# Other block sizes and a crossbar transpose for group 3 in a fused attention and SwiGLU kernel

## The chip, the cores and the metric

The kernel runs on one core of one Trainium2 chip. A core has TensorE (PE in the profile; its weight loads are PEld), VectorE (DVE), ScalarE (ACT), GpSimd (POOL) and SyncE (SP). Each takes its instructions in the order of the program. DMA transfers are issued by SP, ACT or POOL and run on 16 shared DMA engines. The metric is device time in microseconds (us) of one execution; lower is better.

## The reference

Attention with a window of 128 and 4 sink tokens, for 4 batches, 8 heads, 768 positions and a head size of 64; its output, as 3072 tokens of 512, goes through a gated layer with 1536 hidden units.

```python
scores = scale * np.matmul(q, k.transpose(0, 1, 3, 2))
keep = is_sink | in_window          # in_window: 0 <= i - j < 128
scores = np.where(keep, scores, -1000000000.0)
a = np.exp(scores - max);  a = a / (sum + 1e-09)
x = np.matmul(a, v)                 # heads side by side: 3072 x 512
g = x @ w_gate
out = (g * (1.0 / (1.0 + np.exp(-g))) * (x @ w_val)) @ w_out
```

Inputs and output are float32; the kernel computes in bfloat16 with float32 sums.

## The kernel before, in words

**Two tilings.** The attention goes by 12 *groups* of 256 positions, three for each batch (group 3 begins batch 1, group 6 batch 2, group 9 batch 3). The gated layer goes by 8 *blocks* of tokens, whose lengths stand in `SIZES` (L42): 256, 256, 256, 512, 512, 512, 512, 256. A block needs the output of the groups that hold its tokens: block 3 (512) that of groups 3 and 4, block 4 that of 5 and 6, and so on; block 7 (256) that of group 11.

**Attention of a group g.** Keys and queries are loaded as they lie (`load_nat`, four DMAs on POOL's queue, L113) and must be turned so that the head size lies on the partitions. Groups 2 and 3 are turned on TensorE by `step_TN` (L279, four transposes into one PSUM bank `pn`, then a copy by ACT or DVE); from group 4 on by DMA transposes (`xbar`, L293, four issued by SP). The tile that `load_nat` fills has one buffer from group 4 on, so a load waits for the transposes of the group before. `load_v` loads the values. Then:

- `step_S1` (L360): the score matmuls (L382, tile `s`, six PSUM banks), for groups that don't begin a batch also the scores against the sinks (`mm_K`, L432, tile `pk`; with `apart` in `step_S2` instead), three exponentials on ACT (L395) and the first of four masks.
- `step_S2`: three more exponentials, that of the sinks (`es`, L438), and the second mask. `step_S3`: masks 3 and 4. A mask is a multiplication on DVE (L404) over the probabilities `e` of two heads: masks 1 and 2 for heads 0 to 3, masks 3 and 4 for heads 4 to 7.
- `step_PV`, four times a group: the first also issues `step_sinks` (L454 and, from group 4 on in groups that don't begin a batch, L463, over all eight heads); then L494. Each result `o` holds a PSUM bank until DVE has taken its reciprocal (L503) and scaled it into `xn` (L511).
- `step_X`: turns `xn` into `xT`, the gated layer's input, on TensorE for groups 0 to 2 (L543), by a DMA transpose that SP issues from group 3 on (L538).

**A block** is 12 gate units (6 for a block of 256 alone, 8 shared by blocks 0 and 1) and one down unit for each 128 tokens. `gate` (L611): the projection `pg` (L564), tanh on ACT (L584), the attention steps that share the unit, the projection `pv` (L564), then on DVE `u` (L592) and `ht` (L607, L598, L603). The masks that wait in the list `later` go between and behind these two: one behind `u`, the rest behind `ht`; a `flush` among the steps puts them ahead. A step marked `ahead` (`S1`) is issued before `pg`. `down` (L644): 12 matmuls (L657) into a bank `pd`, among which the steps are spread, then a copy by ACT (L662) and a store (L665), issued by ACT for blocks 0 to 2 and by SP for the others. All PSUM tiles share eight banks (L76).

**The order** is written by hand. `weave` runs a list of units and issues with unit i the steps that `slots` gives for i. `one(at, g)` puts `S1` and `S2` at unit `at` and `S3` at the next. The first `weave` (L860) has 24 units: 0 to 11 the gates of blocks 0 and 1, 12 to 17 the gates of block 2, then two downs each of blocks 0 (18, 19), 1 (20, 21) and 2 (22, 23). Blocks 3, 4 and 5 have a `weave` of 16 units each (0 to 11 gates, 12 to 15 downs) with two groups in it (`pair`, L873), blocks 6 and 7 a last one. For block 3 the first gate is split in two halves of 256 tokens, so that it can start on group 3's half.

**Loads** are ordered by POOL's queue. `behind(tb, t)` and `turned(g)` are copies of one element on POOL (L703, L709) that wait for a token of `xT`, or for the queries of group g, and so hold the loads behind them. POOL issues all weights (L162, L169), the last at about 30 us, then keys, queries and values of group 3.

Of the kernel before, what the change touches and what calls it, by code (L numbers as in the profile page):

```python
# [14 lines left out]
def kernel(  # L15
# [12 lines left out]
    nc = tc.nc  # L28
    P = 128
# [9 lines left out]
    NP2 = H // 2  # L39
    GC = S // 256  # L40
    NG = B * GC
    SIZES = [256, 256, 256, 512, 512, 512, 512, 256]  # L42
    assert sum(SIZES) == NTOK and NG == 12
    OFF = [sum(SIZES[:i]) for i in range(len(SIZES))]
    PEX = (0, 1, 2)
# [477 lines left out]
    def step_X(g, j, evict="v"):  # L523
        t0 = g * 256 + j * P
        tb = max(i for i in range(len(SIZES)) if OFF[i] <= t0)
        off = t0 - OFF[tb]
        if tb == 0 and off == 0:
            xTs["01"] = xtp.tile([P, DMC, 512], BF16, tag="xT", name="xT")
            xTs[0], xTs[1] = (xTs["01"][:, :, 256 * i:256 * (i + 1)] for i in range(2))
        elif tb > 1 and off == 0:  # L530
            xTs[tb] = dense(xtp.tile([P, DMC * 512], BF16, tag="xT", name="xT"),
                            DMC, SIZES[tb])
            if tb == 3:
                for i in range(2):
                    xTs[tb, i] = xTs[tb][:, :, 256 * i:256 * (i + 1)]
        if g not in PEX:
            def sp():
                nc.sync.dma_start_transpose(xTs[tb][:, :, off:off + P], xns[g, j])  # L538
            later.append(sp)
            return  # L540
        pt = bank([P, DMC, P], BF16, "px")
        for i in range(DMC):
            nc.tensor.transpose(pt[:, i], xns[g, j][:, i * P:(i + 1) * P], ident)  # L543

        if evict == "a":
            nc.scalar.copy(out=xTs[tb][:, :, off:off + P], in_=pt)
            return

        def dve():
            nc.vector.tensor_copy(out=xTs[tb][:, :, off:off + P], in_=pt)  # L550
        if evict == "now":
            dve()
        else:
            later.append(dve)
# [89 lines left out]
    def down(tb, ts, attn, last=False):  # L644
        at = {}
        for i, a in enumerate(attn):
            at.setdefault(DFC * (i + 1) // (len(attn) + 1), []).append(a)
        n = DFC // 4
        r0 = OFF[tb] + ts * P
        parts = [(0, 3 * P), (3 * P, DM)] if last else [(0, DM)]  # L650
        for m, (lo, hi) in enumerate(parts):
            po = bank([P, hi - lo], FP32, "pd")
            for f in range(DFC):
                for a in at.get(f, []) if m == 0 else []:
                    a()
                    flush()
                nc.tensor.matmul(  # L657
                    po, hts[tb][:, f, ts * P:(ts + 1) * P], wos[f // n][:, f % n, lo:hi],
                    start=(f == 0), stop=(f == DFC - 1))
            ot = opool.tile([P, hi - lo], FP32, tag=f"ot{hi - lo}", name="ot")  # L660
            if m == 0:
                nc.scalar.activation(ot, po, AF.Copy, scale=0.5)  # L662
            else:
                nc.vector.tensor_scalar(ot, po, 0.5, None, op0=ALU.mult)  # L664
            (nc.scalar if tb < 3 else nc.sync).dma_start(out[r0:r0 + P, lo:hi], ot)  # L665

    def gates(tb):
        return [(gate, tb, f) for f in range(0, DFC, 512 // SIZES[tb])]
# [174 lines left out]
    for f in masks1[:3]:  # L843
# [2 lines left out]
    g0, g1, g2 = gates(0), gates(1), gates(2)  # L846
    us = [(gate_held, *g0[0][1:]), (gate_first, *g0[1][1:]), g1[0], g1[1],
          *((gate, "01", f) for f in range(4, DFC)),
          *g2, *downs(0), *downs(1), *downs(2)]

    def L(*fs):
        def f():
# [4 lines left out]
    def NV(g):  # L857
# [3 lines left out]
        (4, TN(2)[::2]), (5, TN(2)[1::2]), ((6, 7), Ss(2)), (6, [K(2)]),  # L861
        ((8, 8), PVs(2)[:2]), (9, [A(step_PV, 2, 0, 1, "a"), A(step_PV, 2, 1, 1, "a")]),
        ((10, 11), [A(step_X, 2, 0, "a"), ahead(A(step_X, 2, 1, "a"))]),
        (11, [NV(4), lambda: nc.gpsimd.tensor_copy(out=vcl[64:128], in_=vcl[0:64])]),
        ((14, 14, 15, 15), TN(3, "aa")),
        (15, [A(xbar, 4)]), (15, [A(load_nat, 5)]), (19, [A(xbar, 5, (0,))]),
        *one(17, 3), (18, [A(step_ks, 1)]), (18, [A(step_vsb, 1)]),
        ((19, 19, 19, 20), PVs(3)), (19, [S1(4)]), (20, [L(A(step_S2, 4), A(step_S3, 4))]), (20, Xs(3)), (20, [A(xbar, 5, (1,))]),
        ((21, 21, 21, 22), PVs(4)), (21, Xs(4)[:1]),
        (22, [Xs(4)[1], flush, A(behind, 3, 511), A(load_v, 5), A(load_nat, 6)]),  # L870
        (23, [A(xbar, 6), A(turned, 6), A(load_v, 6), NV(7)])))

    def pair(ga, gb, at=0):  # L873
        return [*one(at, ga), ((4, 4, 5, 5), PVs(ga)), ((7, 7), Xs(ga)), *one(8, gb, True),
                ((12, 12, 13, 13), PVs(gb)), ((13, 13), Xs(gb))]

    weave([(gate, (3, i), 0) for i in range(2)] + gates(3)[2:] + downs(3), slots(
        (15, [A(step_ks, 2), A(step_vsb, 2)]), *pair(5, 6), (9, [flush, A(xbar, 7)]),
        (13, [flush, A(behind, 4, 511), NV(8)]),
        (15, [A(xbar, 8)]), (15, [NV(9)])))  # L880
    weave(gates(4) + downs(4), slots(
        *pair(7, 8), (3, [A(xbar, 9)]), (15, [A(step_ks, 3), A(step_vsb, 3)]),
        (3, [A(load_nat, 10)]), (13, [flush, A(behind, 5, 511), A(load_v, 10), NV(11)]),
        (15, [A(xbar, 10)])))
    weave(gates(5) + downs(5), slots(*pair(9, 10), (6, [A(xbar, 11)])))
    us = gates(6) + gates(7) + downs(6) + downs(7)
    us[-1] = (lambda tb, t, a: down(tb, t, a, True), *us[-1][1:])
    weave(us, slots(
        *one(0, 11), ((4, 4, 5, 5), PVs(11)), ((8, 9), Xs(11))))


# [33 lines left out]
```

## Time and profile before

| | us |
|---|---|
| median of 3 runs | 234.16 (233.87 to 234.39) |
| the profiled execution | 233.82 |
| its span, first to last instruction | 231.9 |
| TensorE busy | 225.6 |
| DVE busy | 150.9 |
| ACT busy | 106.4 |
| POOL busy | 84.3 |
| mean granted TensorE clock | 0.993 |

Times in the views count from the start of the span. A row of the timeline gives start, duration, engine, line, operation, what it writes and reads, and how often; in brackets how long the engine had been idle and what ended that. The end of a matmul's row is modelled: rows of matmuls that follow each other overlap by about 0.17 us, and the pieces of the chain of waits give the spacing without the overlap. Rows of DVE and ACT overlap by some 0.1 us in the same way, so that their spacing is taken from the starts. "Busy" of TensorE doesn't mean that every matmul is at its peak.

### The profile page before, as it was taken

What the parts mean: (1) busy time and instruction counts of PE and PEld (TensorE: products, weight loads), DVE (VectorE), ACT (ScalarE), POOL (GpSimd) and SP (SyncE); (2) the same over time, 40 slices, a digit from 0 to 9 for tenths busy, and PEclk for the clock granted to TensorE, in tenths of its full rate; (3) what the DMA queues carried; (4) which work ended last, traced back from release to release, by engine and by line L of the source; (5) the groups of instructions that cost most, each with busy time, mean ns of one, the idle gap of its engine ahead of it and who ended that gap; (6) DMA issues with size and microseconds to landing.
All of it is one profiled execution on the core that took longest, in us unless ns stands there. A gap on an engine that the chain in (4) does not pass through costs nothing.

```text
span 231.9 us, 5433 instructions
## 1 busy us (share of the span) xinstructions
PE 225.6 (97%) x2155; PEld 125.4 (54%) x2155; DVE 150.9 (65%) x327; ACT 106.4 (46%) x212; POOL 84.3 (36%) x123
## 2 busy tenths in 40 slices
PE   7699999999999999999999999999999999999994
PEld 3469645796555644455444454454454544487443
DVE  5878888767660797960797970597960599778000
ACT  4784486566543726423635512835612823333221
POOL 8996874960500907806353415135000000000000
PEclk9979999999999999999999999999999999999999
DMA  8999999999998998998989996989915102000132
GB/s 147 150 185 179 179 198 206 164 156 122 123 154 230 103 134 99 151 195 141 146 119 139 128 124 138 105 109 144 117 40 144 45 3 42 3 3 0 64 120 90
DMA packets 112008, 28.04 MB, mean 121 GB/s; under 512 B 99056, under 2 KB 109040, under 8 KB 111984
## 3 DMA queue, kind: packets, MB, share of 16 engines
q0 software_dynamic: 79904, 14.29, 80.7%
q1 hardware_dynamic: 30672, 11.58, 26.7%
q10 hardware_dynamic: 1408, 1.84, 2.5%
q8 instruction: 17, 0.28, 0.5%
q14 instruction: 7, 0.06, 0.1%
HBM read 29.13 MB, written 6.29 MB: 153 GB/s over the span
## 4 chain that ended last, share of the span: by engine, by line
PE 94%; DMA 2%; POOL 2%; DVE 0%; issue 0%; POOLq 0%
PE pg L564 27%; PE pv L564 27%; PE pd L657 27%; PE o L494 4%; PE s L382 3%; DMA rows<-in_q_dram 2%; PE s L326 1%; PE o L463 1%; PE pk L432 1%; PE pn L279 1%; PE o L454 1%; POOL rows L102 1%; POOL x L216 1%; PE px L543 1%; DVE xT L550 0%
## 5 line engine op out<-in xcount | busy, mean ns | idle before, releaser
L592 DVE SCALAR_TENSOR_TENSOR u<-th,pg 128x512 bf16<-128x512 f32 x72 | 49.2, 683 | 45.4 <-ACT th L584 45.1
L564 PE MATMUL pg<-xT,wg 128*128 128x512 bf16 (+1 forms) x360 | 74.2, 337 | 0.3 <-DVE xT L550 0.3
L564 PE MATMUL pv<-xT,wv 128*128 128x512 bf16 (+1 forms) x360 | 74.1, 336 | 0.0
L584 ACT ACTIVATE th<-pg 128x512 f32<-128x512 f32 x72 | 43.7, 608 | 59.6 <-PE pg L564 59.6
L657 PE MATMUL pd<-wo,ht 128*128 128x512 bf16 (+2 forms) x300 | 65.9, 370 | 0.0
L564 PEld LDWEIGHTS <-wg 128*128 128x128 bf16 x360 | 34.4, 98 | 26.7 <-issue 0.7
L564 PEld LDWEIGHTS <-wv 128*128 128x128 bf16 x360 | 33.9, 98 | 23.5 <-issue 0.2
L607 DVE TENSOR_TENSOR ht<-u,pv 128x512 bf16<-128x512 bf16 x62 | 42.5, 686 | 4.7 <-PE pv L564 0.4
L657 PEld LDWEIGHTS <-ht 128*128 128x128 bf16 x300 | 27.5, 98 | 28.4
L662 ACT ACTIVATE ot<-pd 128x512 f32<-128x512 f32 (+1 forms) x24 | 14.3, 595 | 50.2 <-PE pd L657 46.8
L395 ACT ACTIVATE e<-s 128x512 bf16<-128x512 f32 x54 | 28.5, 614 | 5.8 <-PE s L382 4.9
L113 POOL DMA_DIRECT2D nat<-in_k_dram x20 | 17.7, 895 | 29.3 <-DMA qT<-nat 27.8
L511 DVE TENSOR_TENSOR xn<-o,rcp 128x256 bf16<-128x256 f32 x45 | 17.9, 419 | 0.7
L128 POOL DMA_DIRECT2D vm<-in_v_dram x24 | 17.8, 770 | 1.2 <-DMA va<-in_v_dram 0.7
L113 POOL DMA_DIRECT2D nat<-in_q_dram x20 | 17.8, 906 | 1.0 <-DMA wv<-in_moe_w_val_dram 0.5
L494 PEld LDWEIGHTS <-e 128*128 128x128 bf16 x256 | 12.0, 100 | 6.3 <-issue 0.3
L404 DVE TENSOR_TENSOR e<-e,maskq 128x768 bf16<-128x768 bf16 x24 | 13.1, 553 | 1.9 <-ACT e L395 1.9
L151 POOL DMA_DIRECT2D va<-in_v_dram x12 | 10.7, 917 | 4.3 <-DMA wo<-in_moe_w_out_dram 2.4
L703 POOL CAST warmed<-xT 1x1 f32<-1x1 bf16 x3 | 0.5, 175 | 30.2 <-DMA xT<-xn 30.2
L503 DVE RECIPROCAL rcp<-o 128x4 f32<-128x4 f32 x48 | 7.3, 172 | 5.5 <-PE o L494 5.3
L664 DVE TENSOR_SCALAR ot<-pd 128x128 f32<-128x128 f32 x1 | 0.3, 292 | 14.3 <-PE pd L657 14.3
L333 ACT ACTIVATE e<-s 128x512 bf16<-128x512 f32 x16 | 8.3, 607 | 0.6 <-PE s L326 0.5
(86 smaller groups left out, 138.7 us busy)
## 6 DMA issues: line engine op xcount, KB each, us to landing
out_dram<-ot SPq DMA_DIRECT2D x17, 256.0 KB
nat<-in_k_dram POOLq DMA_DIRECT2D x20, 128.0 KB, 4.7
nat<-in_q_dram POOLq DMA_DIRECT2D x20, 128.0 KB, 4.9
va<-in_v_dram POOLq DMA_DIRECT2D x12, 128.0 KB, 5.9
wg<-in_moe_w_gate_dram POOLq DMA_DIRECT2D x6, 256.0 KB, 7.6
wv<-in_moe_w_val_dram POOLq DMA_DIRECT2D x6, 256.0 KB, 8.2
wo<-in_moe_w_out_dram POOLq DMA_DIRECT2D x4, 384.0 KB, 11.1
out_dram<-ot ACTq DMA_DIRECT2D x6, 256.0 KB
```

Source lines behind the costliest of these rows:

```text
L113: nc.gpsimd.dma_start(x[:, i, j].rearrange("p (h d) -> p h d", d=D), src[b, :, t0:t0 + P].rearrange("h p d -> p h d"))
L128: nc.gpsimd.dma_start(vms[b][p0:p1, t - 1, :, 0:D], v[b, :, t0:t0 + p1 - p0].rearrange("h p d -> p h d"))
L395: nc.scalar.activation(e_t[g][:, e0:e0 + 512], pss[g][w, i], AF.Exp, scale=scale)
L404: nc.vector.tensor_tensor(e, e, m.broadcast_to([P, 2, 384]), op=ALU.mult)
L494: nc.tensor.matmul(o, l, r, start=(c == 0 and i == 0), stop=(i == len(mms) - 1), skip_group_check=True)
L511: nc.vector.tensor_tensor(xn, po[:, :, 0:D], rcp.broadcast_to([P, 4, D]), op=ALU.mult)
L564: nc.tensor.matmul(ps[:, i * n:(i + 1) * n], ws[fi][:, c, fo * P:(fo + 1) * P], xTs[tb][:, c], start=(c == 0), stop=(c == DMC - 1))
L584: nc.scalar.activation(th, pg, AF.Tanh, scale=0.5)
L592: nc.vector.scalar_tensor_tensor(u, th, 1.0, pg, op0=ALU.add, op1=ALU.mult)
L607: nc.vector.tensor_tensor(hts[tb][:, f:f + 512 // SIZES[tb]].rearrange("p a n -> p (a n)"), u, pv, op=ALU.mult)
L657: nc.tensor.matmul(po, hts[tb][:, f, ts * P:(ts + 1) * P], wos[f // n][:, f % n, lo:hi], start=(f == 0), stop=(f == DFC - 1))
L662: nc.scalar.activation(ot, po, AF.Copy, scale=0.5)
```

## The change

- `SIZES` becomes 256, 256, 256, 256, 512, 512, 512, 512: group 3 alone feeds block 3, groups 4 and 5 block 4, up to groups 10 and 11 for block 7. What was said of block 3 (the split first gate) holds for block 4, and ACT issues the stores of block 3 too.
- The first `weave` gets eight more units: 24 to 29 the gates of block 3, 30 and 31 its downs.
- Group 3 is no longer turned by `step_TN` in units 14 and 15: `xbar(3)` is issued on SP in unit 12, and in unit 13 `turned(3)` holds POOL's queue until its queries have landed, with the loads of group 4 behind it (they stood in unit 11).
- Group 3's scores move from unit 17 (a gate) to unit 18 (the first down of block 0), the rest of its exponentials and masks to unit 19. Group 4's scores move from unit 19 to unit 23, its values from 21 and 22 to 25 and 26. Group 5's scores stand in unit 27, its values in 29 and 30; before, they stood in units 0, 4 and 5 of block 3's `weave`.
- From block 4 on each `weave` holds the two groups of the next block: 6 and 7, 8 and 9, 10 and 11. The last block's units hold no attention. The small sink steps (`step_ks`, `step_vsb`) of batch 2 go to unit 3 of block 4, those of batch 3 to unit 14 of block 5, and the loads, transposes and holds move with their groups.

```diff
--- before.py
+++ after.py
@@ -39,7 +39,7 @@
     NP2 = H // 2
     GC = S // 256
     NG = B * GC
-    SIZES = [256, 256, 256, 512, 512, 512, 512, 256]
+    SIZES = [256, 256, 256, 256, 512, 512, 512, 512]
     assert sum(SIZES) == NTOK and NG == 12
     OFF = [sum(SIZES[:i]) for i in range(len(SIZES))]
     PEX = (0, 1, 2)
@@ -530,7 +530,7 @@
         elif tb > 1 and off == 0:
             xTs[tb] = dense(xtp.tile([P, DMC * 512], BF16, tag="xT", name="xT"),
                             DMC, SIZES[tb])
-            if tb == 3:
+            if tb == 4:
                 for i in range(2):
                     xTs[tb, i] = xTs[tb][:, :, 256 * i:256 * (i + 1)]
         if g not in PEX:
@@ -662,7 +662,7 @@
                 nc.scalar.activation(ot, po, AF.Copy, scale=0.5)
             else:
                 nc.vector.tensor_scalar(ot, po, 0.5, None, op0=ALU.mult)
-            (nc.scalar if tb < 3 else nc.sync).dma_start(out[r0:r0 + P, lo:hi], ot)
+            (nc.scalar if tb < 4 else nc.sync).dma_start(out[r0:r0 + P, lo:hi], ot)
 
     def gates(tb):
         return [(gate, tb, f) for f in range(0, DFC, 512 // SIZES[tb])]
@@ -846,7 +846,7 @@
     g0, g1, g2 = gates(0), gates(1), gates(2)
     us = [(gate_held, *g0[0][1:]), (gate_first, *g0[1][1:]), g1[0], g1[1],
           *((gate, "01", f) for f in range(4, DFC)),
-          *g2, *downs(0), *downs(1), *downs(2)]
+          *g2, *downs(0), *downs(1), *downs(2), *gates(3), *downs(3)]
 
     def L(*fs):
         def f():
@@ -861,32 +861,33 @@
         (4, TN(2)[::2]), (5, TN(2)[1::2]), ((6, 7), Ss(2)), (6, [K(2)]),
         ((8, 8), PVs(2)[:2]), (9, [A(step_PV, 2, 0, 1, "a"), A(step_PV, 2, 1, 1, "a")]),
         ((10, 11), [A(step_X, 2, 0, "a"), ahead(A(step_X, 2, 1, "a"))]),
-        (11, [NV(4), lambda: nc.gpsimd.tensor_copy(out=vcl[64:128], in_=vcl[0:64])]),
-        ((14, 14, 15, 15), TN(3, "aa")),
-        (15, [A(xbar, 4)]), (15, [A(load_nat, 5)]), (19, [A(xbar, 5, (0,))]),
-        *one(17, 3), (18, [A(step_ks, 1)]), (18, [A(step_vsb, 1)]),
-        ((19, 19, 19, 20), PVs(3)), (19, [S1(4)]), (20, [L(A(step_S2, 4), A(step_S3, 4))]), (20, Xs(3)), (20, [A(xbar, 5, (1,))]),
-        ((21, 21, 21, 22), PVs(4)), (21, Xs(4)[:1]),
-        (22, [Xs(4)[1], flush, A(behind, 3, 511), A(load_v, 5), A(load_nat, 6)]),
-        (23, [A(xbar, 6), A(turned, 6), A(load_v, 6), NV(7)])))
+        (11, [lambda: nc.gpsimd.tensor_copy(out=vcl[64:128], in_=vcl[0:64])]),
+        (12, [A(xbar, 3)]), (13, [A(turned, 3), NV(4)]), (17, [A(xbar, 4), A(load_nat, 5)]),
+        (18, [S1(3)]), (19, [L(A(step_S2, 3), A(step_S3, 3))]),
+        (20, [A(step_ks, 1), A(step_vsb, 1)]),
+        ((20, 20, 21, 21), PVs(3)), (21, Xs(3)), (21, [A(xbar, 5)]),
+        (22, [flush, A(behind, 3, 255), A(load_v, 5), A(load_nat, 6)]),
+        *one(23, 4), ((25, 25, 26, 26), PVs(4)), (26, [A(xbar, 6)]), (26, [A(load_v, 6)]),
+        ((27, 28), Xs(4)),
+        *one(27, 5), ((29, 30, 30, 30), PVs(5)), (30, Xs(5)),
+        (30, [flush, A(behind, 4, 511), NV(7)])))
 
     def pair(ga, gb, at=0):
         return [*one(at, ga), ((4, 4, 5, 5), PVs(ga)), ((7, 7), Xs(ga)), *one(8, gb, True),
                 ((12, 12, 13, 13), PVs(gb)), ((13, 13), Xs(gb))]
 
-    weave([(gate, (3, i), 0) for i in range(2)] + gates(3)[2:] + downs(3), slots(
-        (15, [A(step_ks, 2), A(step_vsb, 2)]), *pair(5, 6), (9, [flush, A(xbar, 7)]),
-        (13, [flush, A(behind, 4, 511), NV(8)]),
-        (15, [A(xbar, 8)]), (15, [NV(9)])))
-    weave(gates(4) + downs(4), slots(
-        *pair(7, 8), (3, [A(xbar, 9)]), (15, [A(step_ks, 3), A(step_vsb, 3)]),
-        (3, [A(load_nat, 10)]), (13, [flush, A(behind, 5, 511), A(load_v, 10), NV(11)]),
-        (15, [A(xbar, 10)])))
-    weave(gates(5) + downs(5), slots(*pair(9, 10), (6, [A(xbar, 11)])))
-    us = gates(6) + gates(7) + downs(6) + downs(7)
+    weave([(gate, (4, i), 0) for i in range(2)] + gates(4)[2:] + downs(4), slots(
+        (3, [A(step_ks, 2), A(step_vsb, 2)]), *pair(6, 7), (2, [A(xbar, 7)]),
+        (7, [flush, A(behind, 5, 255), NV(8)]), (9, [A(xbar, 8)]),
+        (13, [flush, A(behind, 5, 511), NV(9)]), (15, [A(xbar, 9)])))
+    weave(gates(5) + downs(5), slots(
+        *pair(8, 9), (3, [A(load_nat, 10)]), (6, [A(xbar, 10)]),
+        (13, [flush, A(behind, 6, 511), A(load_v, 10), NV(11)]),
+        (14, [A(step_ks, 3), A(step_vsb, 3)]), (15, [A(xbar, 11)])))
+    weave(gates(6) + downs(6), slots(*pair(10, 11)))
+    us = gates(7) + downs(7)
     us[-1] = (lambda tb, t, a: down(tb, t, a, True), *us[-1][1:])
-    weave(us, slots(
-        *one(0, 11), ((4, 4, 5, 5), PVs(11)), ((8, 9), Xs(11))))
+    weave(us, {})
 
 
 # ---- launch: one core; inputs and outputs as the reference has them ----
```

## The prediction

> **What bounds the kernel now.** I read the busy times first, then the chain that ended last, then that chain in order of time, then the queues of VectorE (DVE) and ScalarE (ACT) beside it.
>
> ```profile
> PE 225.6 (97%) x2155; PEld 125.4 (54%) x2155; DVE 150.9 (65%) x327; ACT 106.4 (46%) x212; POOL 84.3 (36%) x123
> ...
> PE 94%; DMA 2%; POOL 2%; DVE 0%; issue 0%; POOLq 0%
> ```
>
> TensorE (PE) is the bound. In stretches of 5 us it is busy for 5.00 of 5.00 from 79 us to 229 us, and the same in stretches of 2 us from 16 us on. So time falls by every TensorE piece that goes, and grows by every wait that TensorE gets. The price of an edit on another engine is nothing until TensorE has to wait for it.
>
> **What goes.** The four transposes of group 3 in units 14 and 15 leave TensorE. The chain in order of time shows them as two pieces:
>
> ```profile
> 47.25 0.45 PE pn L279 x8
> 47.70 0.87 PE pv L564 x8
> 48.57 0.87 PE pg L564 x8
> 49.44 0.45 PE pn L279 x8
> ```
>
> 2 x 0.45 = 0.90 us leaves the path. Their four copies on ACT (0.58 and 0.60 us) go too, worth nothing on an engine that is 46% busy. The new sizes cost nothing by themselves: before and after there are four blocks of 256 and four of 512, and a projection takes 0.87 us (8 matmuls of 256) or 0.86 us (4 of 512).
>
> **What moves on the DMA queues: hidden.** Group 3's keys and queries are issued at 31.48 to 35.54 us and take 12.1 and 11.3 us, so the last lands near 46.9. SP then issues four transposes of 1.2 us as pieces land, the last until 48.1, and they land 1.35 us (86.96 to 88.31) to 3.0 us (127.63 to 130.62) later: 49.5 to 51.1. Behind the new wait on POOL (turned(3), 0.17 us of work) queue group 4's four loads and five loads of values, then group 5's loads; on SP, group 4's transposes. With one buffer each further group waits for the transposes of the one before; that step is
>
> ```profile
> 118.54 1.77 POOL L113 DMA_DIRECT2D nat<-in_k_dram  x2 [6.51 <-DMA qT<-nat]
> ...
> 130.62 1.75 POOL L113 DMA_DIRECT2D nat<-in_k_dram  x2 [6.80 <-DMA qT<-nat]
> ```
>
> 12.1 us. From about 50.4 this gives 62.5 for group 4, 74.6 for 5, 86.7 for 6. Needed: group 3's at 55.13 - 0.90 - 0.87 (its scores leave unit 17: 0.77, and 0.10 on the next matmul) + 6 x 0.216 = 54.7; group 4's in unit 23 at about 68.8; group 5's in unit 27, not before 78. SP then sends group 4's output behind group 6's transposes, near 83.7 to 86.2, landing by 88; block 4 wants it at 90.7 or later. The thinnest cover is 3 to 4 us; past it each us late costs a us.
>
> **What the new order makes TensorE wait for.** This is the step that decides. In unit 24, masks 3 and 4 of group 4 are put into DVE's queue by step_S3, as u, mask, ht, mask; in unit 25 the sinks (L454, L463) read all eight heads. Before, the values came four units after the scores in a gate stretch; now they come two units after (scores 23, values 25; scores 27, values 29). The same two gate units stand in the trace at the head of block 4 (group 7). DVE first, its starts in the first column:
>
> ```profile
> 111.51 0.69 DVE L592 SCALAR_TENSOR_TENSOR u<-th,pg 128x512 bf16<-128x512 f32 x1 [8.34 <-ACT th L584]
> ...
> 113.65 0.68 DVE L592 SCALAR_TENSOR_TENSOR u<-th,pg 128x512 bf16<-128x512 f32 x1
> 114.25 0.55 DVE L404 TENSOR_TENSOR e<-e,maskq 128x768 bf16<-128x768 bf16 x1
> 114.72 0.68 DVE L607 TENSOR_TENSOR ht<-u,pv 128x512 bf16<-128x512 bf16 x1
> 115.32 0.55 DVE L404 TENSOR_TENSOR e<-e,maskq 128x768 bf16<-128x768 bf16 x1
> ```
>
> and TensorE:
>
> ```profile
> 111.55 1.03 PE L564 MATMUL pg<-xT,wg 128*128 128x512 bf16 x4
> ...
> 117.69 0.29 PE L454 MATMUL o<-vsb,es 32*128 32x260 bf16 x4
> 117.91 0.45 PE L463 MATMUL o<-vm,e 64*64 64x65 bf16 x32
> ```
>
> The unit with S3 starts its pg at 111.55; its last mask ends at 115.32 + 0.55 = 115.87, 4.32 us later. TensorE, unhindered, wants heads 4 to 7 after pg, pv, pg (3 x 0.865), L454 (0.22) and half of L463 (0.19): 3.00 us after that start. Here nobody minds, since the sinks come at 117.69.
>
> *Group 5* (units 27, 28, 29: this very form): wait 4.32 - 3.00 = **1.3 us**.
>
> *Group 4* (scores in the last down): I walk from the start of unit 24. The down with scores lasts 12 x 0.216 + 0.82 + 0.22 + 0.10 = 3.73. ACT's seven exps begin 1.31 after its start (4 x 0.216 + 0.45) and take 6 x 0.485 + 0.15, so they end 0.64 after unit 24 begins. Then comes the down's own copy, and its store, which ACT issues:
>
> ```profile
> 73.79 0.60 ACT L662 ACTIVATE ot<-pd 128x512 f32<-128x512 f32 x1 [1.99 <-PE pd L657]
> 74.42 0.34 ACTq L665 DMA_DIRECT2D out_dram<-ot  x1
> 74.86 1.57 ACT L395 ACTIVATE e<-s 128x512 bf16<-128x512 f32 x3 [0.47 <-PE pk L432]
> ```
>
> 1.07 from copy to the next work. The last row names pk, which ended at 74.80; the store's issue ended at 74.76, and for group 7 the same exps start (109.36) before pk (109.58), so I take the store. So tanh runs from 1.71 to 2.33, u at 2.37, mask +0.61, ht +0.47, mask +0.60, end +0.55: 4.60. TensorE is there at 3.02: wait **1.6 us**. Were ACT free at once it would be 0.9; if the store didn't hold ACT, 1.0.
>
> *Banks.* A score step takes six of the eight PSUM banks, the last two from two thirds of its 0.82 us on (0.55). Before, it always had a unit without values ahead of it, or downs. Unit 27 follows directly on the values of unit 26. At its start pg, pv and two o banks are held; DVE frees them in order (u 1.7 after unit 26 starts, +0.61, two reciprocals +0.18, ht +0.60 and 0.09 to its end, then xn): the sixth bank is free 1.2 us into unit 27: wait 0.65, and 0.05 for the sinks' scores, together **0.7** (bounds 0 to 1.0). In block 4 the sinks of batch 2 (0.77 us of DVE, 102.30 to 103.10 without the memset) move from the last down, where DVE idles, into gate unit 3, and ACT's stores of block 3 hold its start back 0.5 (pg to u: 2.2 in the old block 3, 1.7 in the old block 4). In the old block 5 (same groups' form) the ht ahead of the score step ends at 159.96, 0.1 us before scores at 160.06; 1.27 us later it makes the sixth bank wait 0.6, and a pv in unit 5 some 0.15: **0.75** (bounds 0 to 1.0).
>
> **The sum.** -0.90 + 1.6 + 1.3 + 0.7 + 0.75 = **+3.45 us**. The same walk along the old order finds no wait, and DVE's lag at the end of units 0, 1, 2 of the old block 3 as 2.6, 3.1, 2.7 us against 2.6, 3.0, 2.65 in the trace, so the steps are good to about 0.1; what is not shown is how banks are dealt out. Bounds: waits of 0.9 + 1.0 + 0 + 0 = 1.9 to 1.7 + 1.7 + 1.0 + 1.0 = 5.4, net +1.0 to +4.5. The profiled run took 233.82 us (231.9 span, 1.9 around it), 0.34 below the median 234.16. 233.82 + 3.45 = 237.27; with the median's excess about **237.5**.
>
> **The clock.** One view could make it worse (columns: stretch; busy us and count of PE, PEld, DVE, ACT, POOL; granted clock; DMA):
>
> ```profile
> 9.00:10.00 1.00, 0.45 (x16) 0.22 (x8) 0.96 (x2) 1.00 (x4) 1.00 (x3) 1.00 2.22 161
> ...
> 12.00:13.00 1.00, 1.00 (x18) 0.67 (x13) 0.66 (x3) 0.62 (x2) 1.00 (x3) 0.50 1.91 161
> ```
>
> After two short gaps the clock fell to half from 11.4 to 14.8 us, worth 0.29 + 0.50 + 0.50 + 0.42 = 1.7 us of work. The gaps were 0.31 and 0.78 us, among matmuls of 64 x 64. A wait of 1.6 us among full matmuls is longer, but the rest of its surroundings is dense, so I don't put a fall into the sum; I keep it as a rival. The Trainium skill, "TensorE: Matmul & The Clock Gate", "Part 1: The HAM clock gate", has the clock fall only after an idle window of about 3.4 us, by which neither wait would cost a fall; the rows above show a fall after much shorter gaps. By the page the sum stays +3.45, by the rows it could be 5.15.
>
> **Rivals.**
> *(a) Only the data waits, at their smallest*: ACT's store doesn't hold tanh (group 4 waits 1.0), banks fall free in time: 1.0 + 1.3 - 0.9 = +1.4, 235.6 with the median's excess. For it: bank waits of this kind are nowhere in the trace. Against: 74.42 shows the store holding ACT.
> *(b) The clock falls once*: +1.7 on the forecast, less what the later waits then shrink (some 0.5): 238.7; twice, 240.
> *(c) Faster*: the place is the last mask of units 24 and 28. If both end before TensorE's 3.0 us, only -0.90 is left: 233.3, -0.4%. It decides at 0.90 us of waits in all: below, the kernel is faster, above, slower. For it: no TensorE wait shows anywhere in the steady part, and DVE is only 65% busy. Against: u, mask, ht, mask stand in order on one queue and even with ACT free at once take 0.9 too long in unit 24 and 1.3 in unit 28, by rows.
> *(d) The transposes come late*: were the links 14 instead of 12.1 us (the first took 15, 42.45 to 57.48, behind the weights), group 5's would land near 79.8, after 78, and group 6's would push block 4's input to about 92; the waits above give most of that cover back. 0 to 2 us more, 238.5. That the change doesn't do what it says is covered here: a late xbar(3) moves the stall to unit 18.
>
> **How the numbers follow.** Forecast 0.62, its own range 236.3 to 238.6; (a) 0.14; (b) 0.12; (c) 0.08; (d) 0.04. From 235.3 to 239.3 leaves out (c), half of (b) and some of (a). About 0.2% (0.5 us) is what a measurement here can tell from no change: (c) gives faster 0.07, and 0.03 lies within, where (a) and (c) meet; slower 0.90.
>
> **What would show it.** Right: no `pn` of group 3 between 46 and 52 us and unit 18 early by 1.8; TensorE idle some 1.6 us inside the L463 group of group 4 near 75 us, ended by DVE's L404; 1.3 us inside that of group 5 near 86; shorter gaps ahead of scores (L382) near 80 and in the middle of block 4. Wrong: TensorE without a gap from 60 to 115 us (then (c)); waits ended by a DMA (d); a granted clock of 0.5 after 75 us (b). The forecast falls if masks are taken ahead of u in DVE's queue.

## The result, and the profile after

The changed kernel takes **249.06 us** (median of 6 runs, 248.65 to 251.5) against 234.01 (6 runs, 232.92 to 234.55) on the same chip: ratio 1.067, 95% interval 1.062 to 1.072. The direction was forecast, the size was not: 15.1 us more instead of 3.3, and above the range. The profiled execution took 251.5 us, its span is 249.7. Two of the kernels further down (group 3 first, in the new order) also had executions in a slower state; their times are the medians of the others.

The page of the kernel after first: the busy times, the granted clock in 40 slices of 6.2 us, and the chain that ended last.

```profile
PE 227.7 (91%) x2114; PEld 126.6 (51%) x2139; DVE 152.5 (61%) x327; ACT 105.0 (42%) x208; POOL 85.0 (34%) x125
...
PEclk9999999999968779999999999999999999999999
...
PE 51%; DMA 27%; POOL 10%; DVE 4%; issue 3%; SPq 2%; ACT 1%; POOLq 0%; ACTq 0%; DVEq 0%
```

Three things are new. TensorE's share fell from 97 to 91%. The clock has a dent from slice 12 to slice 15. And the chain, which was TensorE for 94%, now runs through DMA for 27% and POOL for 10%: that is the form of loads that wait for each other, not of an engine's queue. From the waits view (us in total, times, longest us):

```profile
POOL nat L113 <- DMA qT<-nat: 25.7, 3, 12.1
...
PE o L463 <- DVE e L404: 6.4, 4, 4.6
...
PE s L382 <- DMA qT<-nat: 5.6, 2, 4.1
ACT th L584 <- DMA kT<-nat: 5.2, 1, 5.2
```

The same row of before:

```profile
POOL nat L113 <- DMA qT<-nat: 27.8, 4, 8.4
```

The last three rows are new: TensorE waits for masks and for turned queries (groups 4 and 7), and ACT for turned keys. POOL waited for transposes before too; what is new is that one of its waits is 12.1 us long, where the longest of before was 8.4.

Now POOL's timeline of the kernel after (start, duration, and in brackets how long the engine stood and what ended it):

```profile
48.94 0.34 POOL L864 COPY vcl<-vcl 64x195 f32<-64x195 f32 x1 [6.23 <-DMA kT<-nat]
...
53.09 0.18 POOL L709 CAST warmed<-qT 1x1 f32<-1x1 bf16 x1 [3.81 <-DMA qT<-nat]
53.34 1.76 POOL L113 DMA_DIRECT2D nat<-in_k_dram  x2
...
56.88 3.86 POOL L128 DMA_DIRECT2D vm<-in_v_dram  x5
72.81 1.76 POOL L113 DMA_DIRECT2D nat<-in_k_dram  x2 [12.07 <-DMA qT<-nat]
```

And that of the kernel before, with the loads of group 4 and, at 57.48, of group 5:

```profile
42.45 1.75 POOL L113 DMA_DIRECT2D nat<-in_k_dram  x2
...
57.48 1.75 POOL L113 DMA_DIRECT2D nat<-in_k_dram  x2 [6.13 <-DMA qT<-nat]
```

The hold, turned(3), ends at 53.1, so group 4's loads start at 53.34 instead of 42.45, 10.9 us later. The hold itself accounts for the last 3.8 us of that. For 6.2 us before it POOL stood at the copy of the sink rows (L864), which in the kernel before came behind group 4's loads and now comes ahead of them. The link of group 4's loads, from the first load of group 4 to the first of group 5, is 72.81 - 53.34 = 19.5 us long. Group 4 is turned at 72.3 then, and TensorE has stood since 68.3:

```profile
72.39 1.49 PE L382 MATMUL s<-qT,kT 64*64 64x192 bf16 x52 [4.11 <-DMA qT<-nat]
...
85.16 0.27 PE L463 MATMUL o<-vm,e 64*64 64x65 bf16 x4 [4.56 <-DVE e L404]
86.22 0.38 PE L463 MATMUL o<-vm,e 64*64 64x65 bf16 x12 [0.80 <-DVE e L404]
```

The second row is the place where I had forecast 1.6 us. It is named as a wait for a mask, but most of it is not the mask's own. ACT's timeline there:

```profile
77.54 0.60 ACT L662 ACTIVATE ot<-pd 128x512 f32<-128x512 f32 x1 [1.21 <-PE pd L657]
82.87 0.34 ACTq L665 DMA_DIRECT2D out_dram<-ot  x1
83.31 1.09 ACT L584 ACTIVATE th<-pg 128x512 f32<-128x512 f32 x2 [5.17 <-DMA kT<-nat]
```

The copy of block 2's second down is done at 78.14, its store is issued only at 82.87, and both tanh of the next block stand behind it in ACT's queue. It waits for a transpose of group 5's keys, which a store of outputs has nothing to do with. The semaphores that the trace records with each DMA say why. The DMAs that SP and ACT issue in these kernels share eight completion semaphores, which are used again and again. The store's had last been used by the second of group 5's two kT transposes. That one was issued at 78.44 and landed at 82.80, and 0.07 us later the store was issued. The kT transposes came from 76.38 on, because group 5's loads came 19.5 us after group 4's.

Last, the stretches (us; busy us and count of PE, PEld, DVE, ACT, POOL; granted clock; DMA; GB/s). Of the kernel after:

```profile
48.00:52.00 4.00, 4.00 (x39) 3.59 (x37) 3.15 (x6) 1.19 (x2) 0.34 (x1) 1.00 0.40 77
52.00:56.00 4.00, 3.95 (x37) 2.26 (x37) 2.13 (x4) 2.08 (x4) 2.84 (x5) 1.00 0.50 49
...
72.00:76.00 4.00, 3.28 (x64) 2.21 (x66) 1.12 (x2) 2.88 (x6) 3.19 (x4) 0.50 0.96 141
...
84.00:88.00 4.00, 2.05 (x29) 1.55 (x30) 3.13 (x7) 0.40 (x1) 3.67 (x5) 0.50 0.84 86
```

The same two first stretches of the kernel before:

```profile
48.00:52.00 4.00, 4.00 (x43) 3.64 (x41) 2.67 (x4) 2.74 (x6) 2.60 (x4) 1.00 2.47 154
52.00:56.00 4.00, 4.00 (x44) 2.87 (x43) 2.40 (x4) 3.40 (x8) 0.00 (x0) 1.00 2.43 166
```

The DMA column (a mean over the 16 engines of packet time, which passes 1 where packets overlap) falls from 2.4 to 0.4 and 0.5: while POOL stands at the sink copy and at the hold, the DMA engines have little to do, from 48 to 55 us. And the clock is at half from 70.3 to 77.1 and from 84.0 to 90.8 us, during and after each long wait.

The account of the profiled run: span +17.8. TensorE's busy time is +2.1, which is -0.9 (no `pn` of group 3) and some +3.0 from the lower clock (what is left, not a row). Its idle time goes from 6.3 to 22.0, +15.7; of this 13.0 are 4.11 (scores 4), 4.56 + 0.80 (masks 4), 1.08 (masks 5), 0.31 and 0.33 (banks), 1.49 (scores 7) and 0.33 behind scores 4. 1.0 is a wait for weights at the start, which has nothing to do with the change: every other trace but that of before has it too (0.4 to 1.2), also those of two kernels in the old order.

### The profile page after: what moved, and what is told of

It is laid out like the page before. It is cut to its first block, busy times and chain, and to the rows that moved or that the text cites. A ratio compares the mean times of both kernels' runs of the same rounds, so it can differ in the third digit from the quotient of the medians.

```text
span 249.7 us, 5391 instructions
## 1 busy us (share of the span) xinstructions
PE 227.7 (91%) x2114; PEld 126.6 (51%) x2139; DVE 152.5 (61%) x327; ACT 105.0 (42%) x208; POOL 85.0 (34%) x125
## 3 DMA queue, kind: packets, MB, share of 16 engines
q0 software_dynamic: 79904, 14.29, 77.1%
## 4 chain that ended last, share of the span: by engine, by line
PE 51%; DMA 27%; POOL 10%; DVE 4%; issue 3%; SPq 2%; ACT 1%; POOLq 0%; ACTq 0%; DVEq 0%
PE pd L657 17%; PE pg L564 15%; PE pv L564 15%; DMA qT<-nat 8%; DMA nat<-in_q_dram 5%; DMA wo<-in_moe_w_out_dram 4%; POOL nat L113 4%; DMA wv<-in_moe_w_val_dram 3%; DMA nat<-in_k_dram 2%; DMA vcl<-in_v_dram 2%; PE s L382 2%; SPq L293 2%; DMA kT<-nat 2%; PE o L494 2%; POOL va L151 2%
## 5 line engine op out<-in xcount | busy, mean ns | idle before, releaser
L564 PEld LDWEIGHTS <-wg 128*128 128x128 bf16 x360 | 34.9, 99 | 28.1 <-DMA wg<-in_moe_w_gate_dram 1.2
L564 PEld LDWEIGHTS <-wv 128*128 128x128 bf16 x360 | 34.4, 99 | 24.7 <-issue 0.6
L395 ACT ACTIVATE e<-s 128x512 bf16<-128x512 f32 x54 | 28.5, 610 | 12.5 <-PE s L382 11.6
L113 POOL DMA_DIRECT2D nat<-in_k_dram x20 | 17.8, 897 | 28.5 <-DMA qT<-nat 25.7
L404 DVE TENSOR_TENSOR e<-e,maskq 128x768 bf16<-128x768 bf16 x24 | 13.2, 554 | 10.9 <-ACT e L395 10.9
L703 POOL CAST warmed<-xT 1x1 f32<-1x1 bf16 x5 | 0.9, 173 | 54.3 <-DMA xT<-xn 54.3
L113 POOL DMA_DIRECT2D nat<-in_q_dram x20 | 17.8, 908 | 1.1 <-DMA wg<-in_moe_w_gate_dram 1.0
L128 POOL DMA_DIRECT2D vm<-in_v_dram x24 | 17.8, 785 | 0.1
L382 PE MATMUL s<-qT,kT 64*64 64x64 bf16 (+4 forms) x366 | 8.7, 229 | 5.9 <-DMA qT<-nat 5.6
L382 PEld LDWEIGHTS <-kT 64*64 64x64 bf16 (+1 forms) x366 | 7.0, 113 | 9.8 <-issue 9.7
```

The costliest lines, as they stand in the source:

```text
L113: nc.gpsimd.dma_start(x[:, i, j].rearrange("p (h d) -> p h d", d=D), src[b, :, t0:t0 + P].rearrange("h p d -> p h d"))
L128: nc.gpsimd.dma_start(vms[b][p0:p1, t - 1, :, 0:D], v[b, :, t0:t0 + p1 - p0].rearrange("h p d -> p h d"))
L382: nc.tensor.matmul(pss[g][w, lo // 8][part, 64 * (lo % 8):64 * (lo % 8) + 64 * (hi - lo)], kTs[b][r, p, k0:k0 + kn], qTs[b][r, p, cc:cc + ...
L395: nc.scalar.activation(e_t[g][:, e0:e0 + 512], pss[g][w, i], AF.Exp, scale=scale)
L564: nc.tensor.matmul(ps[:, i * n:(i + 1) * n], ws[fi][:, c, fo * P:(fo + 1) * P], xTs[tb][:, c], start=(c == 0), stop=(c == DMC - 1))
```

## The experiments

Four theories. **A**: group 4's loads start 11 us late, and with one buffer the chain of groups 4, 5, 6 has no room. **B**: the new order alone, values two units after scores, with the masks behind u and ht. **C**: the store on ACT stands still on a shared semaphore. **D**: a transpose by the crossbar lands late when loads run beside it. Unless a line says otherwise, each edit is made on the kernel after. Before took 233.2 to 233.6 beside these runs.

### The order alone: group 3 on TensorE again, group 4's loads at their old place

```diff
-(12, [A(xbar, 3)]), (13, [A(turned, 3), NV(4)]), (17, [...])
+((14, 14, 15, 15), TN(3, "aa")), (17, [...])      # NV(4) in unit 11
```

> Edit: group 3 is turned on TensorE again in units 14 and 15 (0.90 us back on TensorE, four copies back on ACT), with group 4's loads in unit 11 as in the kernel before; sizes and all later places stay as in the changed kernel. Theory A: as the run with early loads, plus 0.9 us, since SP's queue and the crossbar are free for group 4 still earlier: 240 to 243. Theory B: the waits of 1.6 and 1.3 us and the bank waits stay: 238 to 240. If the crossbar transposes of group 3 were the trouble by themselves, this run would come down to 234 to 235 and the run with early loads would not.

**238.59 us**, ratio 1.023 (1.019 to 1.026). No DMA wait before group 7, no wait of ACT on a DMA, and the clock stays at full speed. TensorE's waits:

```profile
75.12 0.22 PE L463 MATMUL o<-vm,e 64*64 64x65 bf16 x4 [0.46 <-DVE e L404]
76.19 0.29 PE L463 MATMUL o<-vm,e 64*64 64x65 bf16 x12 [0.84 <-DVE e L404]
80.77 0.45 PE L382 MATMUL s<-qT,kT 64*64 64x128 bf16 x17 [0.47 <-DVE ht L607]
87.23 0.22 PE L463 MATMUL o<-vm,e 64*64 64x65 bf16 x4 [0.84 <-DVE e L404]
87.70 0.29 PE L463 MATMUL o<-vm,e 64*64 64x65 bf16 x12 [0.25 <-DVE e L404]
106.07 1.02 PE L564 MATMUL pv<-xT,wv 128*128 128x512 bf16 x4 [0.29 <-DVE ht L607]
111.36 0.90 PE L382 MATMUL s<-qT,kT 64*64 64x192 bf16 x52 [0.81 <-DMA qT<-nat]
```

1.30 + 0.47 + 1.09 + 0.29 + 0.81 = 3.96 us. The order costs 5.0 us by the medians, some 4 of them in these rows. So some 10 of the 15 us lie elsewhere.

### Only the late loads: group 3 on TensorE, group 4's loads held until 53

```diff
+def held_by(tb, f):
+    nc.gpsimd.tensor_copy(out=warmed[0:1], in_=hts[tb][0:1, f, 0:1])
-(12, [A(xbar, 3)]), (13, [A(turned, 3), NV(4)]), (17, [A(xbar, 4), ...])
+((14, 14, 15, 15), TN(3, "aa")),
+(17, [A(held_by, 2, 9), NV(4), A(xbar, 4), ...])
```

> The kernel after with group 3 on TensorE (no transpose of it by the crossbar at all), but group 4's loads held back by POOL until unit 16's ht is written, near 53, where the kernel after has them (53.3). Theory A (the loads of group 4 start 11 us late and the chain of one buffer behind them has no room): group 4's scores wait 2 to 4 us for qT, the store on ACT stands still again, the clock falls: 244 to 248, against 238.6 with the loads at 42. Theory D (the crossbar's own transposes of group 3 are the cost): 238 to 240.

**248.87 us**, ratio 1.067 (1.059 to 1.076): the time of the kernel after, without one transpose of group 3 by the crossbar. POOL and TensorE of this run:

```profile
53.28 1.76 POOL L113 DMA_DIRECT2D nat<-in_k_dram  x2
...
70.53 0.89 POOL L113 DMA_DIRECT2D nat<-in_k_dram  x1 [9.84 <-DMA qT<-nat]
```

```profile
70.11 0.89 PE L382 MATMUL s<-qT,kT 64*64 64x192 bf16 x52 [1.25 <-DMA qT<-nat]
...
82.76 0.27 PE L463 MATMUL o<-vm,e 64*64 64x65 bf16 x4 [6.60 <-DVE e L404]
```

The loads start at 53.28, as in the kernel after, and the link is 17.2 us. TensorE waits less for group 4's scores and more behind ACT's store (ACT stands 6.62 us there): the sum is set by when the chain delivers group 5, not by where TensorE waits for it. Theory A holds: this one start, 11 us later, is worth 248.87 - 238.59 = **10.3 us**, and with the 5.0 of the order that makes 15.3 of the 15.1 measured. The 0.9 us of `pn`, on TensorE again in this run, makes no visible difference (248.87 against 249.06).

### Early loads with the crossbar

```diff
+(11, [NV(4), ...]), (12, [A(xbar, 3)]), (13, [A(turned, 3)])
```

> Edit: group 4's nine loads go back to unit 11, ahead of turned(3), so that nothing holds them. Theory A (the loads of group 4 start 11 us late, at 53.3 us instead of 42.5, and each later group hangs on the one before through the single buffer): group 4's queries land near 60 instead of 72.3, the wait of 4.1 us ahead of group 4's scores goes, group 5's keys land before the last store of block 2 is issued, so the 5.2 us that ACT stood still there go too, and the clock does not fall. Time 240 to 242. Theory B (the values stand too near to their scores, whatever the loads do): the waits of TensorE in units 25 and 29 shrink only to the 1.6 and 1.3 us of the prediction, so some 3 to 4.5 us above the kernel before stay: 237 to 239. Theory C (the store that ACT issues is the cause): without change in it, ACT still stands still and the time stays above 245.

**245.41 us**, 1.050 (1.046 to 1.055): more than A or B has room for, and not by C's reason, since TensorE waits for no store here (ACT stands 2.4 and 2.2 us at DMAs ahead of copies). Group 4's scores are in time, and the wait is now one group earlier:

```profile
58.29 1.46 PE L382 MATMUL s<-qT,kT 64*128 64x256 bf16 x18 [4.43 <-DMA qT<-nat]
```

Group 3's queries land near 58 instead of 53.0, since group 4's nine loads run beside their transposes. The clock falls behind this wait too, to half from 56.7 us on. So the hold is not the fault in itself: with it group 4 is late, without it group 3.

### The part alone in the old order

The kernel before, with one edit:

```diff
-((14, 14, 15, 15), TN(3, "aa")),
+(12, [A(xbar, 3)]),
```

> The kernel before (old sizes, old order) with one thing changed: group 3's keys and queries go through the crossbar, issued in unit 12, and group 4's loads start in unit 11 as they did before. Theory D (a transpose by the crossbar lands late when loads issued by POOL run beside it): group 3's last piece lands near 58 as with the early loads, its scores in unit 17 wait 4 to 4.5 us, group 4's scores in unit 19 wait another 0 to 2, 0.9 us of TensorE goes: 237.5 to 239.5, with a fall of the clock up to 241. Theory A (only the late start of group 4's loads hurts): no wait above 1 us, 232.7 to 234.5. The prediction's row of 1.35 to 3.0 us for a transpose gives scores without a wait and 233.0.

**242.39 us**, 1.038 (1.033 to 1.043). The scores of group 3 come at unit 17, with TensorE ready at 51.1:

```profile
58.11 1.46 PE L382 MATMUL s<-qT,kT 64*128 64x256 bf16 x18 [6.97 <-DMA qT<-nat]
```

The landing near 58 was as theory D had it; TensorE was ready earlier than I had put it, so the wait is 7.0 and not 4 to 4.5. Sizes and order have no share in these 9 us.

### Group 3 first of all, in the old order and in the new

The kernel before, with group 3's loads ahead of the output weights and its transposes ahead of the sink loads on SP:

```diff
-for i in range(4): load_out(i)
-load_nat(3); load_v(3)
+load_nat(3)
+for i in range(4): load_out(i)
+load_v(3); xbar(3)
-((14, 14, 15, 15), TN(3, "aa")),
```

> The kernel before (old sizes, old order) with group 3 turned by the crossbar, but its loads go ahead of the four loads of the output weights, and its transposes ahead of the sink loads on SP, so that they are done before group 4's loads are issued. Theory D (transposes are late only because they run beside group 4's loads and hold up the chain behind them): group 3 is turned by 46 to 50, no wait in its scores, group 4's transposes land near 55, 0.9 us of TensorE goes: 232.0 to 233.2, against 242.4 with the same part issued behind all weights. If a transpose of group 3 beside any loads is the cost, the weights' loads hurt as much: 236 to 241.

**238.63 us**, 1.023 (1.019 to 1.027): better than 242.39 by 3.8, but not below before. Group 3 is in time now (0.50 us, ended by DVE), and group 4 is late:

```profile
61.98 1.15 PE L382 MATMUL s<-qT,kT 64*64 64x192 bf16 x52 [2.38 <-DMA qT<-nat]
```

Theory D's time (232.0 to 233.2) is missed, and the time lies in the range of its rival. The rival is right about group 3: its four transposes, issued at 36.5 to 40.8, landed at 44.6 to 51.5, 8.0 to 11.4 us later, beside the output weights. TensorE asked at 51.2, so a part of its 0.50 us may be theirs. Group 4 is late because its loads now run beside the output weights too: its first load was issued at 40.93 and landed 12.8 us later, against 7.4 in the kernel before, so SP could issue its first transpose only at 53.75 instead of 49.81. In the old order the chain has no 2 us to give either. The same two edits on the kernel after:

> The kernel after with group 3's loads ahead of the output weights and its transposes ahead of the sink loads on SP; sizes, order, stores as after. The hold then ends at once and group 4's loads start near 43. Theory A and D together (a late, slow chain): no wait on kT or qT before group 7, the store on ACT finds its semaphore free, and what the order costs stays: the run with group 3 on TensorE, 238.6, less 0.9, so 237 to 238.5. If the store on ACT stands still by itself, 241 to 244.

**249.93 us**, 1.073 (1.069 to 1.077): a miss, by a wait that I had not seen. POOL's copy of the sink rows stands ahead of the hold, and the eight sink loads, now behind the transposes on SP, come late (SP takes 10.1 us to issue them, 2.7 in the kernel before): POOL stands there 12.9 us, and group 4's loads start at 54.0. The time is again that of loads near 53. With the same edits, group 4's scores a unit earlier, group 5's masks ahead of u and the stores on SP:

> As the one before, with group 4's scores one unit earlier (in block 2's first down instead of its second, its values in units 24 and 25), masks of group 5 ahead of u in unit 28, stores of blocks 2 and 3 on SP. Theory B with bank waits: values two units after scores cost 1.30 + 1.09 in L463 and the scores of group 5 behind group 4's values 0.5 to 1.7 for a bank; all go, the 0.8 of group 7 and 0.3 of pv may stay, 0.9 goes with the transposes: 232.7 to 234.3. If the order costs elsewhere, 235 to 237.

**244.21 us**, 1.049 (1.045 to 1.052). POOL of this run, and its first late scores:

```profile
53.44 0.35 POOL L865 COPY vcl<-vcl 64x195 f32<-64x195 f32 x1 [12.69 <-DMA vcl<-in_v_dram]
...
53.98 1.76 POOL L113 DMA_DIRECT2D nat<-in_k_dram  x2
```

```profile
70.99 1.49 PE L382 MATMUL s<-qT,kT 64*64 64x192 bf16 x52 [4.62 <-DMA qT<-nat]
```

Both runs fail as tests of an early group 3, but both agree with A: with the loads at 54, asking for group 4 a unit earlier only makes TensorE wait longer.

### Values out of the way of group 4's transposes

```diff
-(13, [A(turned, 3), NV(4)]), (17, [A(xbar, 4), A(load_nat, 5)])
+(13, [A(turned, 3), A(load_nat, 4)]),
+(17, [A(xbar, 4), A(load_nat, 5), A(load_v, 4)])
```

> The kernel after with the five loads of group 4's values moved behind group 5's loads of keys and queries, so that none of them runs beside group 4's transposes. Theory D: group 4's queries land by 62.5 or earlier, its transposes 2 to 4 us later instead of 9.4, near 66.5, its scores no longer wait 4.1 us, the link to group 5 shrinks from 19.5 to 13 us, and the store on ACT waits less: 240 to 243. Theory A (late start alone): the transposes land where they did, within 1 us, and 247 to 249 stays. Theory C (the store on ACT alone): 247 to 249.

**248.87 us**, 1.064 (1.058 to 1.069). POOL shows what D had foretold:

```profile
53.31 1.76 POOL L113 DMA_DIRECT2D nat<-in_k_dram  x2
...
66.90 1.77 POOL L113 DMA_DIRECT2D nat<-in_k_dram  x2 [10.08 <-DMA qT<-nat]
```

Group 4 is turned at 66.4 instead of 72.3, the link is 13.6 instead of 19.5 us, and the scores don't wait. From its issue to its landing the last transpose took 9.37 us in the kernel after (from 62.88) and 4.60 here (from 61.75). But the values themselves are now late (L463 waits 6.2 us in all for `vm`, the longest 3.3), so the time shows no gain and misses D's 240 to 243: what was taken from one transfer was given to the next.

### The masks ahead of u

```diff
+(24, [flush]), ..., (28, [flush])
```

> Edit: a flush in units 24 and 28, which puts masks 3 and 4 of groups 4 and 5 ahead of u in DVE's queue. Theory B (masks behind u and ht make TensorE wait in L463): the waits of 5.4 and 1.1 us in L463 go and the time falls by 5 to 6 us, to 243 to 244. Theory A (late loads): u of unit 24 still comes only after ACT's stall, near 83.9 us; TensorE gets past L463 but runs out of banks one or two units later, so most of the 5.4 us comes back: a gain of 1 to 2 us, 247 to 248. Theory C (ACT's store): the same as A, 247 to 248.

**244.44 us**, 1.046 (1.043 to 1.050). No wait in L463 is left; in its place TensorE waits 3.24 us for u, since ACT's store stands 5.68 us as before. The gain of 4.6 us lies between B's 5 to 6 and the 1 to 2 of A and C. On the run with group 3 on TensorE, where no store stands, the same edit:

> The sizes and the order of the kernel after, group 3 on TensorE with group 4's loads early (as in the run with group 3 on TensorE, 238.6), and the masks of groups 4 and 5 ahead of u in units 24 and 28. Theory B (the sinks wait because masks 3 and 4 stand behind u and ht): the waits of 1.30 and 1.09 us in L463 go, 0 to 0.5 comes back as a wait for u: 236.2 to 236.8. If the order costs in another place, 238 to 239.

**235.85 us**, 1.009 (1.006 to 1.012): 2.7 less than 238.59, of which 1.30 + 1.09 are the waits for masks. Two waits for a bank are left, 0.47 at group 5's scores and 1.67 at group 7's; with 0.16 behind scores 4 they are 2.3 of the remaining 2.5 us. With group 4's scores and values a unit earlier as well (scores 22, values 24 and 25, masks of group 5 ahead of u):

> Group 3 on TensorE and group 4's loads early (238.6), with group 4's scores one unit earlier, values in units 24 and 25, masks of group 5 ahead of u in unit 28. Theory B with bank waits: the waits of 1.7 and 0.5 us for a bank that the run with masks ahead still had (235.85) go as well: 233.3 to 234.8. If those waits come from the sizes and not from the closeness of group 5's scores to group 4's values, 235.5 to 236.5.

**235.58 us**, 1.010 (1.007 to 1.013). From 60 to 94 us TensorE doesn't wait at all, so the wait at group 5's scores did come from group 4's values right ahead of them; the time stays above B's 234.8 for another reason. What is left:

```profile
94.60 1.03 PE L564 MATMUL pg<-xT,wg 128*128 128x256 bf16 x8 [0.55 <-ACT th L584]
109.63 0.89 PE L382 MATMUL s<-qT,kT 64*64 64x192 bf16 x52 [2.04 <-DMA qT<-nat]
```

2.59 us against 2.4 by the medians. Most of it is group 7's, whose loads stand behind a wait for block 4's input (L703, until 94.59). So there is nothing in these runs that the new sizes by themselves cost.

### The stores of blocks 2 and 3 on SP

```diff
-(nc.scalar if tb < 4 else nc.sync).dma_start(...)
+(nc.scalar if tb < 2 else nc.sync).dma_start(...)
```

> Edit: SP issues the stores of blocks 2 and 3, not ACT. Theory C (ACT stands still for 5.2 us, from 77.5 to 82.8, because its store of block 2's last down waits for a transfer of SP's, and tanh and u queue behind it): tanh of unit 24 comes at about 78.5, the wait in L463 shrinks from 5.4 to the predicted 1.6 us and the clock does not fall a second time; the wait for group 4's queries (4.1) stays: 243 to 245. Theory A: the stalled store now holds SP's queue and with it group 6's transposes instead; less than 2 us gained, above 247. Theory B: the wait in L463 is the masks' own, so nothing is gained: 249.

**242.17 us**, 1.037 (1.031 to 1.042): 6.9 less than the kernel after, more than C had asked. ACT no longer waits for a DMA in the steady part, and of the masks' waits the ordinary ones are left:

```profile
70.12 1.18 PE L382 MATMUL s<-qT,kT 64*64 64x192 bf16 x52 [2.14 <-DMA qT<-nat]
78.45 0.29 PE L463 MATMUL o<-vm,e 64*64 64x65 bf16 x12 [0.69 <-DVE e L404]
...
89.50 0.22 PE L463 MATMUL o<-vm,e 64*64 64x65 bf16 x4 [0.84 <-DVE e L404]
```

With the masks ahead of u too:

> The kernel after with the stores of blocks 2 and 3 on SP and the masks of groups 4 and 5 ahead of u. If the costs add (stores 6.9, masks 2.7): 239 to 240, with group 4's scores still waiting about 2 us for qT and group 7's about 1. If the one hides the other: 241 to 242.5.

**242.57 us**, 1.039 (1.033 to 1.047), no gain. The masks' waits are gone, and group 5's scores wait instead:

```profile
82.39 0.89 PE L382 MATMUL s<-qT,kT 64*64 64x192 bf16 x52 [2.33 <-DMA qT<-nat]
```

While the chain is late, TensorE's other waits only shift the time at which it meets the chain. With the values moved as well:

> All three at once on the kernel after: values of group 4 behind group 5's keys and queries, stores of blocks 2 and 3 on SP, masks ahead of u in units 24 and 28. If A's late chain, B, C and D are all there is: only the bank wait of group 5 (0.47), pv (0.3) and group 7's late queries (0.8 to 1.5) are left against the 0.9 that goes: 234.5 to 236. If a late start alone decides, group 4's scores still wait 2 to 4 us: 238 to 240.

**242.94 us**, 1.039 (1.032 to 1.046): above both ranges. The scores of groups 4 and 5 wait 0.16 us at most, but the late values, which I had counted in neither range, take 5.6 us, and the clock is at half from 78.4 to 85.2 us.

## Why the prediction was wrong, step by step

**What goes: right, but worth nothing here.** No `pn` of group 3 is in the trace; with the chain late, the 0.9 us did not reach the end.

**What moves on the DMA queues: this step failed.** It said that the chain stays hidden behind a cover of 3 to 4 us, with links of 12.1 us. The first term was nearly good: group 3 is turned at 53.0, 2 us past my bound of 51.1, and 1.7 ahead of the need that I had put. (SP issued the first of the four transposes at 45.84, and the four took it 6.0 us, not 4.8, so the last was out at 51.8 and not at 48.1; it landed 1.2 us later.) The next term was mis-sized: group 4's link measured **19.5 us, not 12.1**. I took 12.1 from 118 to 130 us, where two loads of values followed the four; behind group 4 stand five, and they run beside its transposes. The link of my own trace with that company was the first one, 42.45 to 57.48, 15 us; I named it in rival (d) and blamed the weights. Without the values the link measured 13.6. From 53.3, 15 us end at 68.3, just when TensorE asks; the measured 17.2 to 19.5 end at 70.5 to 72.8. So the cover wasn't thin, it was nothing. That the chain starts 11 us later than before is worth 10.3 of the 15.1 us, as the run with late loads shows.

**Two consequences that I didn't price.** I let ACT's store hold ACT for the 0.5 us of its issue; it stood 5.2 us, because a late transpose of group 5 held its semaphore. The kernel before had such a place, and I didn't look at it: there ACT's copy of block 1's first down ends at 65.55, and its store is issued at 68.62, 0.08 us after a kT transpose of group 5 with the same semaphore landed; TensorE did not wait there, so it cost nothing. And I priced a late chain at 0 to 2 us; it cost 10.3, as the run with late loads alone shows. Moving the stores gives back 6.9 of it. The waits of 4 us and more also halved the clock, twice for 6.8 us.

**What the order makes TensorE wait for: right.** Measured without the late chain: group 4's masks 1.30 (1.6 forecast), group 5's 1.09 (1.3), the bank at group 5's scores 0.47 (0.7), pv 0.29 (0.15). At group 7's scores it was 0.81 for late queries, not 0.6 for a bank. 3.96 against 4.35 forecast, and 5.0 by the medians: some 1 us of it is in no row that I can name. Had the chain been hidden, the kernel would have come out 0.9 below the 238.59 of that run, some 237.7 by estimate; no run shows that. My 237.5 was the time of a kernel that its DMA queues didn't allow. Three slips of the working change nothing: the last stretch of 5 us before 229 is busy for 4.97 and not 5.00, 237.27 and 0.34 make 237.6, and 88 against 90.7 leaves block 4's input a cover of 2.7 us, not 3 to 4.

**The rivals.** (d) was the right one, with 4% and a price five times too small. (b), the clock, came true as a consequence of (d). (a) and (c) both needed the chain in time.

**What stays open.** Whether some other order of loads lets the crossbar turn group 3 for nothing. No version that I ran beats the kernel before; the nearest (235.58 and 235.85) have group 3 on TensorE.

## What to carry to other kernels

Work taken off the bound and put on a queue is free only if the whole chain behind it, down to the last group that shares its buffer, still arrives in time: walk that chain with link lengths taken where the same loads stood beside it, and compare the start of each with before. A hold on a queue delays all that is queued behind it: here, with the sink copy ahead of it, it left the DMA engines with little to do for 7 us, and the loads behind it paid that time. When waits of several kinds follow from one late chain, removing one of them shifts the rest; only putting the chain back in time shows what each is worth.

## What the runs showed of the hardware that I had not expected

*A store can wait for an unrelated transpose.* ACT stood 4.7 to 7.8 us behind the store of block 2's last down in five runs (5.2 in the kernel after), and in none of the four that issue this store on SP. In the other runs that issue it on ACT it went out within 0.1 us of its copy's end. The Trainium skill, "DMA: Bandwidth & Descriptors", "Anatomy of one DMA — SWDGE (gpsimd) path", says that a wait on a semaphore takes place at the sequencer that issues the DMA, before it is dispatched; the ACT rows agree: everything behind the store on that engine stood too.

*A transpose's landing depends on its company*. From issue to landing, the last of a group's four took 9.4 us beside five loads of values and stores (group 4 in the kernel after), 4.6 without the values (group 4 with the values moved), 10.8 beside the output weights (group 3 first, old order), and 2.4 (85.75 to 88.19) to 3.6 (126.41 to 130.05) in the steady part of the kernel before.

*The clock falls after shorter waits than 3.4 us.* The Trainium skill, "TensorE: Matmul & The Clock Gate", "Part 1: The HAM clock gate", asks for an idle window of about 3.4 us. TensorE waits of 2.14 us (store on SP), 2.33 (with the masks) and 2.38 us (group 3 first) were each followed by a clock of 0.50. The half clock then lasted 3.4 us each time (70.6 to 74.0, 83.7 to 87.1 and 62.4 to 65.8), which is the length that the page gives for a window, and is worth 1.7 us.

The length of a wait alone doesn't decide it, though: waits of 2.04 us (masks ahead, group 4 a unit earlier), 2.30 us (ahead of group 7's scores, stores on SP and masks ahead) and even 2.89 us (the same place, group 3 first with stores on SP) were followed by full clock, and by the same small matmuls of a score step. Where a wait lies does. In all 16 traces the changes of the granted clock lie a whole number of 3.41 us apart. Cut into such windows from one change on, TensorE's rows between 17 and 225 us give this: at full clock, each of the 15 windows in which it stood idle for 2.08 us or more was followed by half clock, and none with 1.89 us or less was. The 2.14 us lay in one window, the 2.89 us were cut into 1.42 and 1.47 by the end of one. In the first 17 us this count doesn't hold: 1.15 us idle in a window were followed by half clock in the kernel before, and by full clock in the kernel after.
